# A dense layer's forward and backward pass on one core: an edge column copied on chip instead of loaded, a bias row spread by TensorE, and the orders written anew

## The chip, the core and the metric

The kernel runs on one core of a Trainium2 chip. The core has five engines with a queue each: TensorE (PE, matrix products; its weight loads are listed as PEld), VectorE (DVE), ScalarE (ACT), GpSimd (POOL) and SyncE (SP). Transfers run on 16 DMA engines and are issued from the queues of SyncE, ScalarE and GpSimd. The metric is device time in microseconds (us). Before the change three runs took 267.77, 268.63 and 269.6 us; the median is 268.63.

## The reference

x and grad_out are 2048 x 448, w1 is 448 x 1792, w2 is 1792 x 448, all in bf16. The kernel computes the layer and all its gradients:

```python
def _fwd_reference(x, w1, b1, w2, b2):
    h = jnp.einsum("bsd,df->bsf", x, w1) + b1
    h = _gelu(h)                      # tanh form
    return jnp.einsum("bsf,fd->bsd", h, w2) + b2
# reference: out, and the gradients of x, w1, b1, w2, b2 for grad_out
```

## The kernel before

The 2048 rows are cut into 4 blocks of 512, the 1792 hidden columns into 14 tiles of 128, worked on in pairs: 4 x 7 = 28 pairs, numbered p = 0 to 27. The work has two stages. The first goes through the blocks and computes the output and x's gradient; the second computes the gradients of w1 and w2 from the whole of x and grad_out. The change touches the first stage and the loads ahead of it.

No scheduler decides the order. Each engine has a written list of short names (`PE_ORDER`, `ACT_ORDER`, `DVE_ORDER`, `SP_ORDER`), and the class `Plan` turns the names into instructions in that order. Every operation names the values that it reads and writes; the waits follow from that. An engine does its list strictly in order, so an operation that waits holds up all behind it.

The names on TensorE. `W10` is ten warm-up products of constants. `h0`, `h1` are the first pair's product x w1 for the two halves of block 0. `u3.1` and `u3.2` are the two runs of the same product for pair 3, `q3.1` and `q3.2` those of grad_out w2 transposed. The last 64 of the 448 rows are folded in: a run keeps the upper and the lower 64 rows of the array busy with different halves, three slots of two products in run 1 and four in run 2. For that the first 64 numbers of each row stand a second time, in partitions 64 to 127 one column ahead of the transposed block. The transposed load fills that place with numbers of the row before; for block 0 there is none, so a small load (`+x` for x, `+g` for grad_out, function `LED`) brings the column. Run 2 of u and of q reads it. `p2.0` to `p2.3` are parts of the output of block 0 for pair 2. `o1.0.0.6.1` is a part of the output of block 1: row half 0, hidden tiles 0 to 6, run 1; `x...` is the same for x's gradient.

The names on VectorE and ScalarE. `c3A` and `c3B` move the two PSUM banks of u3 to SBUF with the bias b1, on whichever engine the list puts them. Then follow the steps of gelu and its derivative: `s` (square) and `g` (gelu) and `t` (tanh) on ScalarE, `e r y z m n` on VectorE, and `G`, which multiplies with q's result in PSUM. Since q has only one pair of banks (`qb`), the next q waits for G. `vo1.2` moves a part of the output out of PSUM and adds b2 (VectorE); `vx1.2` moves a part of x's gradient, on either engine.

The names on SyncE and ScalarE's queue for loads. `X0.0`, `X0.1`: the two halves of x's block 0, transposed; `Y0`: block 0 of grad_out; `L0` to `L3`: four column parts of w1 (256, 256, 512 and 768 columns), rows 0 to 383; `R0`, `R1`: the last 64 rows of w1; `R2`, `R3`: its first 64 rows a second time, which run 2 reads. `K0` to `K3`: parts of w2, wanted by the p parts; `J` w2 transposed, wanted by q; `I` w1 transposed, wanted by x's gradient; `b2`: the bias loaded once for each of the 128 partitions. Stores are `H`, `T` and `S`; `Nx` and `Ng` load x and grad_out for the second stage. Stores to the outputs go through three staging buffers (`stage`).

Of the kernel before, what the change touches and what calls it, by code (L numbers as in the profile page):

```python
# [88 lines left out]


PE_ORDER = """
W10 h0.0 h1.0 u1.1 u2.1 u1.2 u2.2 u3.1 p0.0 p0.1 u3.2 u4.1 p0.2 p0.3 u4.2 p1.0 p1.1 p1.2 p1.3 u5.1 p2.0 p2.1 u5.2 p2.2
p2.3 p3.0 p3.1 q0.1 p3.2 p3.3 u6.1 q0.2 u6.2 p4.0 p4.1 q1.1 p4.2 p4.3 q1.2 p5.0 p5.1 p5.2 p5.3 u7.1 q2.1 u7.2 q2.2
p6.0 p6.1 u8.1 p6.2 p6.3 u8.2 q3.1 x0.1.0.6.1 u9.1 q3.2 u9.2 x0.0.0.6.1 q4.1 u10.1 q4.2 u10.2 x0.0.0.6.2 q5.1 u11.1
q5.2 u11.2 x0.1.0.6.2 x0.0.6.10.1 u12.1 q6.1 u12.2 q6.2 x0.1.6.10.1 x0.0.6.10.2 u13.1 q7.1 u13.2 q7.2 x0.1.6.10.2
x0.0.10.14.1 q8.1 x0.1.10.14.1 u14.1 q8.2 u14.2 x0.0.10.14.2 q9.1 x0.1.10.14.2 u15.1 q9.2 u15.2 o1.0.0.6.1 q10.1 u16.1
q10.2 u16.2 o1.1.0.6.1 o1.0.0.6.2 u17.1 q11.1 u17.2 q11.2 o1.1.0.6.2 o1.0.6.10.1 o1.1.6.10.1 u18.1 q12.1 u18.2 q12.2
o1.0.6.10.2 u19.1 o1.1.6.10.2 u19.2 o1.0.10.14.1 o1.1.10.14.1 q13.1 u20.1 q13.2 u20.2 o1.0.10.14.2 o1.1.10.14.2 q14.1
x1.0.0.6.1 q14.2 x1.1.0.6.1 x1.0.0.6.2 x1.1.0.6.2 q15.1 x1.0.6.10.1 q15.2 x1.1.6.10.1 u21.1 x1.0.6.10.2 u21.2
x1.1.6.10.2 q16.1 x1.0.10.14.1 u22.1 q16.2 u22.2 x1.1.10.14.1 x1.0.10.14.2 x1.1.10.14.2 u23.1 q17.1 u23.2 q17.2  # L100
o2.0.0.6.1 o2.1.0.6.1 u24.1 q18.1 u24.2 q18.2 o2.0.0.6.2 o2.1.0.6.2 o2.0.6.10.1 o2.1.6.10.1 q19.1 u25.1 q19.2 u25.2
o2.0.6.10.2 o2.1.6.10.2 o2.0.10.14.1 o2.1.10.14.1 q20.1 o2.0.10.14.2 u26.1 q20.2 u26.2 o2.1.10.14.2 x2.0.0.6.1 q21.1
x2.1.0.6.1 q21.2 x2.0.0.6.2 u27.1 x2.1.0.6.2 u27.2 q22.1 x2.0.6.10.1 q22.2 x2.1.6.10.1 x2.0.6.10.2 x2.1.6.10.2 q23.1
x2.0.10.14.1 q23.2 x2.1.10.14.1 x2.0.10.14.2 x2.1.10.14.2 q24.1 o3.0.0.6.1 q24.2 o3.1.0.6.1 o3.0.0.6.2 o3.1.0.6.2
q25.1 o3.0.6.10.1 q25.2 o3.1.6.10.1 o3.0.6.10.2 o3.1.6.10.2 q26.1 o3.0.10.14.1 q26.2 o3.1.10.14.1 o3.0.10.14.2 q27.1
o3.1.10.14.2 q27.2 x3.0.0.6.1 x3.1.0.6.1 x3.0.0.6.2 x3.1.0.6.2 x3.0.6.10.1 x3.1.6.10.1 x3.0.6.10.2 x3.1.6.10.2
x3.0.10.14.1 x3.1.10.14.1 x3.0.10.14.2 x3.1.10.14.2
"""
ACT_ORDER = """
L0 R0 b1 table c0A0 c0A1 s0 g0 c1A t0 s1 g1 s2 g2 c4A g3 g4 t1 t2 s3 c5A g5 s4 s5 c6A g6 t3 s6 c7A t4 g7 c8A c8B g8 s7  # L110
t5 c9A c9B g9 s8 t6 c10A c10B g10 s9 t7 c11A c11B g11 s10 t8 c12A c12B g12 s11 t9 c13A c13B g13 s12 t10 c14A c14B
vx0.1 g14 s13 c15A c15B g15 t11 t12 c16A c16B g16 s14 t13 c17A s15 c17B g17 s16 t14 c18A c18B g18 s17 c19A c19B t15
g19 s18 c20A c20B g20 t16 s19 t17 s20 c21A c21B t18 g21 s21 c22A c22B vx1.0 t19 g22 vx1.3 c23A s22 c23B g23 t20 s23
c24A c24B t21 g24 s24 c25A c25B t22 g25 s25 c26A c26B t23 g26 t24 c27A s26 c27B s27 g27 t25 vx2.0 vx2.2 t26 t27 vx3.0
vx3.2
"""
DVE_ORDER = """
b1T c0B0 c0B1 e0 r0 y0 c1B z0 c2A c2B m0 c3A c3B e1 e2 r1 c4B z1 r2 y1 z2 y2 n0 c5B m1 m2 n1 n2 G0 c6B e3 r3 y3 z3 G1
m3 e4 n3 r4 y4 z4 c7B G2 m4 vo0.2 vo0.3 vo0.0 vo0.1 e5 n4 r5 y5 z5 G3 m5 e6 n5 r6 y6 z6 G4 m6 e7 n6 r7 y7 z7 G5 m7 e8
n7 r8 y8 z8 m8 G6 n8 e9 r9 y9 z9 G7 m9 e10 n9 r10 y10 z10 G8 m10 vx0.0 e11 n10 vx0.2 vx0.3 r11 G9 z11 e12 y11 r12 y12  # L120
z12 m11 G10 m12 e13 n11 r13 y13 z13 n12 m13 G11 n13 e14 r14 y14 z14 m14 n14 G12 e15 r15 y15 z15 m15 n15 G13 e16 vo1.0
vo1.1 vo1.2 vo1.3 r16 y16 z16 G14 m16 e17 n16 r17 y17 z17 m17 G15 n17 e18 r18 y18 z18 m18 n18 G16 e19 r19 y19 z19
vx1.1 vx1.2 m19 n19 G17 e20 r20 y20 z20 m20 n20 G18 e21 r21 y21 z21 m21 n21 G19 e22 r22 y22 z22 vo2.0 m22 vo2.1 G20
n22 vo2.2 vo2.3 e23 r23 y23 z23 G21 e24 m23 r24 y24 z24 n23 m24 n24 G22 e25 r25 y25 z25 m25 G23 n25 vx2.1 e26 vx2.3
r26 y26 z26 G24 m26 e27 n26 r27 y27 z27 m27 n27 G25 G26 vo3.0 vo3.1 vo3.2 vo3.3 G27 vx3.1 vx3.3
"""
# [33 lines left out]
def make_plan(tc, ctx, x, w1, b1, w2, b2, grad_out, out_0, out_1, out_2, out_3, out_4, out_5):  # L160
    nc = tc.nc
    P = 128
# [199 lines left out]
    def wake(n):  # L362
        def fn():
            for i in range(n):
                nc.tensor.matmul(bk_(0), lhsT=one[:, 0:P], rhs=one, start=True, stop=True, skip_group_check=True)
# [238 lines left out]
    for eng, order in (("ACT", ACT_ORDER), ("DVE", DVE_ORDER)):  # L604
        for t in order.split():
            k, a = t[0], t[1:]
            if k == "c":
                hf = None if a[-1] in "AB" else int(a[-1])
                a = a if hf is None else a[:-1]
                C(int(a[:-1]), "AB".index(a[-1]), eng, hf)  # L610
            elif k == "v":
                EV(a[0], *num(a[1:]), eng)
            elif k == "L":
                LW1(int(a), eng)
            elif k == "R":
                LW1R(int(a), eng)
            elif t in ("+x", "+g"):
                LED({"x": "xT", "g": "gT"}[a], 0, eng)
            elif k == "K":
                LW2(int(a), eng)  # L620
            elif t == "b1":
                dma(eng, "b1", b1n[0:NF, :], b1.rearrange("(f p) -> f p", p=P), ["b1z"], ["b1n"], 3584)
            elif t == "b1T":
                pl.op(eng, "b1T", b1_turn, ["b1n"], ["b1T"], ("tiny", 4))
            elif t == "table":
                pl.op(eng, "table", lambda: nc.scalar.activation(out=tiny[:], in_=one[:, 0:1], func=ACT.Gelu_apprx_tanh), [], ["tiny"], ("table", 1))
# [167 lines left out]
```

## Time and profile before

| | |
|---|---|
| median of three runs | 268.63 us |
| profiled execution | 269.21 us |
| its span | 267.4 us |
| mean granted TensorE clock | 0.992 |
| TensorE busy | 260.8 us (98%) |
| VectorE busy | 196.1 us (73%) |
| ScalarE busy | 128.8 us (48%) |
| chain that ended last | PE 95%, DMA 2%, SPq 2% |

The span is what the profile shows of the execution; 1.8 us of its time lie outside. The chain that ended last is followed back from the last instruction, at each step to what released it; an engine's share in it is the time in which the end of the kernel hung on that engine. A timeline row gives start, duration, engine, source line, operation, what it writes and reads, and in brackets the idle time before it with what ended it. The granted clock of TensorE is 1.00 at full speed and 0.50 at half. A line ending in "Q" (SPq, ACTq) is an engine's queue issuing a transfer.

### The profile page before, as it was taken

What the parts mean: (1) busy time and instruction counts of PE and PEld (TensorE: products, weight loads), DVE (VectorE), ACT (ScalarE), POOL (GpSimd) and SP (SyncE); (2) the same over time, 40 slices, a digit from 0 to 9 for tenths busy, and PEclk for the clock granted to TensorE, in tenths of its full rate; (3) what the DMA queues carried; (4) which work ended last, traced back from release to release, by engine and by line L of the source; (5) the groups of instructions that cost most, each with busy time, mean ns of one, the idle gap of its engine ahead of it and who ended that gap; (6) DMA issues with size and microseconds to landing.
All of it is one profiled execution on the core that took longest, in us unless ns stands there. A gap on an engine that the chain in (4) does not pass through costs nothing.

```text
span 267.4 us, 5276 instructions
## 1 busy us (share of the span) xinstructions
PE 260.8 (98%) x2156; PEld 150.5 (56%) x2156; DVE 196.1 (73%) x273; ACT 128.8 (48%) x163; POOL 15.2 (6%) x9
## 2 busy tenths in 40 slices
...
GB/s 165 281 207 200 174 162 196 91 317 241 205 289 156 237 223 162 82 192 120 78 150 146 297 140 39 247 187 107 162 174 198 192 174 170 165 214 196 69 71 34
DMA packets 121705, 46.20 MB, mean 173 GB/s; under 512 B 99054, under 2 KB 121551, under 8 KB 121680
## 3 DMA queue, kind: packets, MB, share of 16 engines
...
q0 software_dynamic: 64, 0.01, 0.0%
...
## 4 chain that ended last, share of the span: by engine, by line
PE 95%; DMA 2%; SPq 2%; issue 0%; ACT 0%
PE bank L238 47%; PE qb L238 16%; PE bank L750 12%; PE bank L696 11%; PE qb L696 5%; PE qb L750 4%; DMA w1f<-in_w_dram 2%; SPq L513 1%; SPq L501 1%; ACT w_sb L755 0%
## 5 line engine op out<-in xcount | busy, mean ns | idle before, releaser
L238 PEld LDWEIGHTS <-HG 64*128 64x128 bf16 x896 | 56.4, 94 | 31.3 <-POOLq L233 0.9
L238 PE MATMUL qb<-gT,w2Tf 64*128 64x512 bf16 x392 | 52.9, 376 | 0.0
L238 PE MATMUL bank<-xT,w1f 64*128 64x512 bf16 x364 | 50.1, 387 | 1.7 <-DMA w1f<-in_w_dram 1.7
L238 PE MATMUL bank<-w_sb,HG 64*128 64x448 bf16 x448 | 48.0, 349 | 0.0
L238 PE MATMUL bank<-w1T_sb,HG 64*128 64x448 bf16 x448 | 47.3, 349 | 0.0
L464 DVE SCALAR_TENSOR_TENSOR HG<-TR,qb 128x1024 bf16<-128x1024 bf16 x28 | 34.1, 1216 | 5.9 <-PE qb L238 5.7
L750 PEld LDWEIGHTS <-HG 128*128 128x128 bf16 x240 | 23.4, 98 | 19.2
L238 PEld LDWEIGHTS <-w1f 64*128 64x128 bf16 x378 | 22.1, 96 | 20.9 <-DMA w1f<-in_w_dram 2.5
L238 PEld LDWEIGHTS <-w2Tf 64*128 64x128 bf16 x392 | 24.2, 94 | 16.6
L449 ACT ACTIVATE TR<-TR 128x1024 bf16<-128x1024 bf16 x28 | 29.3, 1049 | 8.7 <-DVE TR L439 8.6
L696 PEld LDWEIGHTS <-gh_nat 128*128 128x128 bf16 x224 | 21.8, 98 | 20.6 <-issue 0.4
L750 PE MATMUL bank<-w2Tf,HG 128*128 128x448 bf16 (+1 forms) x176 | 32.3, 344 | 0.0
L696 PE MATMUL bank<-w1f,gh_nat 128*128 128x448 bf16 x160 | 30.8, 353 | 0.0
L719 DVE TENSOR_TENSOR w1T_sb<-w1T_sb,gh_nat 128x1792 f32<-128x1792 f32 x14 | 28.4, 2026 | 0.5
L454 DVE TENSOR_SCALAR TR<-TR 128x2048 bf16<-128x2048 bf16 x28 | 19.2, 688 | 8.2 <-ACT TR L449 8.2
L725 POOL PARTITION_ALL_REDUCE w1T_sb<-w1T_sb x1 | 10.6, 10649 | 209.5 <-DVE w1T_sb L723 209.5
L424 ACT ACTIVATE TR<-gh_nat 128x1024 bf16<-128x1024 bf16 x15 | 15.7, 1052 | 8.5 <-DVE TR L459 8.5
L406 ACT ACTIVATE ub<-bank,b1T 128x512 bf16<-128x512 f32 (+1 forms) x22 | 14.0, 673 | 11.8 <-PE bank L238 5.4
L459 DVE TENSOR_TENSOR TR<-TR 128x1024 bf16<-128x1024 bf16 x28 | 19.1, 685 | 0.3
L444 DVE TENSOR_TENSOR TR<-TR,HG 128x1024 bf16<-128x1024 bf16 x28 | 19.1, 682 | 0.0
L756 DVE CAST w_sb<-bank 128x448 bf16<-128x448 f32 x5 | 3.1, 623 | 19.9 <-PE bank L750 19.9
L701 ACT ACTIVATE TR<-bank 128x448 bf16<-128x448 f32 x10 | 5.4, 544 | 24.1 <-PE bank L696 22.0
...
## 6 DMA issues: line engine op xcount, KB each, us to landing
...
out_dram<-st SPq DMA_DIRECT2D x16, 224.0 KB, 2.4
...
out_dram<-xT SPq DMA_DIRECT2D x2, 384.0 KB, 3.0
...
w1f<-in_w_dram SPq DMA_DIRECT2D x1, 576.0 KB, 5.9
```

What stands on the lines that cost most here:

```text
L238: m = nc.tensor.matmul(bk_(b)[:, 0:n], lhsT=l, rhs=r, start=st, stop=sp, skip_group_check=True)
L406: fn = lambda: nc.scalar.activation(out=out, in_=src, func=ACT.Identity, bias=bias)
L424: pl.op("ACT", f"s{p}", lambda: nc.scalar.activation(out=TR[p % NTR][:, 1], in_=ubuf(p), func=ACT.Square, scale=sc), [("ub", p)], [v], ("a ...
L444: pl.op("DVE", f"R{p}", lambda: nc.vector.tensor_tensor(out=t[:, 1], in0=t[:, 1], in1=hblk(p), op=ALU.mult), [("r", p), ("h", p)], [val((" ...
L449: pl.op("ACT", f"t{p}", lambda: nc.scalar.activation(out=t[:, 0], in_=t[:, 0], func=ACT.Tanh), [("y", p)], [val(("t", p), ("TR0", p % NTR) ...
L454: pl.op("DVE", f"m{p}", lambda: nc.vector.tensor_scalar(out=t[:], in0=t[:], scalar1=1.0, scalar2=None, op0=ALU.subtract), [("t", p), ("r2" ...
L459: pl.op("DVE", f"n{p}", lambda: nc.vector.tensor_tensor(out=t[:, 0], in0=t[:, 0], in1=t[:, 1], op=ALU.mult), [("m0", p), ("m1", p)], [val( ...
L464: pl.op("DVE", f"G{p}", lambda: nc.vector.scalar_tensor_tensor(out=ghblk(p), in0=t[:, 0], scalar=2.0, in1=qb[:, :, :], op0=ALU.subtract, o ...
L696: nc.tensor.matmul(bk_(bk)[:, 0:D], lhsT=gh_nat[:, st // 4, ft, st % 4, :], rhs=x_nat[:, st, :], start=(st == 0), stop=(st == NS - 1))
L719: nc.vector.tensor_tensor(out=hs3, in0=a, in1=gh_nat[:, st // 4, :, st % 4, :], op=ALU.add)
L725: pl.op("POOL", "gb1", lambda: nc.gpsimd.partition_all_reduce(gb1_w, hsum, channels=P, reduce_op=bass_isa.ReduceOp.add), ["hsc"], ["gb1"], ...
L750: nc.tensor.matmul(bk_(bk)[:, 0:d1 - d0], lhsT=h_nat[ft][:, st, :], rhs=g_nat[:, st, d0:d1], start=(st == 0), stop=(st == NS - 1))
```

## The change

- `+x` and `+g` leave SyncE's list. `Dx0` and `Dg0` take their place in VectorE's list: a copy of one column of the transposed block from partitions 0 to 63 into partitions 64 to 127.
- b2 is loaded as one row of 448 numbers into the first partition of a staging buffer, from ScalarE's queue behind b1 and ahead of the table load. TensorE spreads it over 128 partitions by a product with ones (`B`, into bank 3), and VectorE copies it out of PSUM (`b2c`).
- The warm-up is nine products, then B, then one more product.
- All four lists are new. In SyncE's, L2 follows R2 directly, L3 goes behind K1, K0, R1 and R3, and Y0, J0 and X1 follow K3. In TensorE's, q0 starts after u6, the output of a block comes ahead of x's gradient of the block before, and the parts of o and x are cut in 4, 4, 3 and 3 hidden tiles instead of 6, 4 and 4. ScalarE takes nearly all first halves of u (`cA`) and all of `vx`; VectorE takes all second halves from pair 4 on (`cB`).

```diff
 PE_ORDER = """
-W10 h0.0 h1.0 u1.1 u2.1 u1.2 u2.2 u3.1 p0.0 p0.1 u3.2 u4.1 p0.2 p0.3 u4.2 p1.0 p1.1 p1.2 p1.3 u5.1 p2.0 p2.1 u5.2 p2.2
-p2.3 p3.0 p3.1 q0.1 p3.2 p3.3 u6.1 q0.2 u6.2 p4.0 p4.1 q1.1 p4.2 p4.3 q1.2 p5.0 p5.1 p5.2 p5.3 u7.1 q2.1 u7.2 q2.2
+W9 B W1 h0.0 h1.0 u1.1 u2.1 u1.2 u2.2 u3.1 p0.0 p0.1 u3.2 u4.1 p0.2 p0.3 u4.2 p1.0 p1.1 p1.2 p1.3 p2.0 u5.1 p2.1 p2.2
+u5.2 p2.3 p3.0 p3.1 p3.2 u6.1 p3.3 u6.2 q0.1 p4.0 p4.1 q0.2 p4.2 u7.1 p4.3 p5.0 u7.2 p5.1 p5.2 p5.3 u8.1 p6.0 p6.1
+u8.2 q1.1 p6.2 p6.3 q1.2 u9.1 o1.1.0.4.1 u9.2 o1.0.0.4.1 q2.1 u10.1 q2.2 u10.2 o1.0.0.4.2 q3.1 u11.1 q3.2 u11.2
...
 ACT_ORDER = """
-L0 R0 b1 table c0A0 c0A1 s0 g0 c1A t0 s1 g1 s2 g2 c4A g3 g4 t1 t2 s3 c5A g5 s4 s5 c6A g6 t3 s6 c7A t4 g7 c8A c8B g8 s7
-t5 c9A c9B g9 s8 t6 c10A c10B g10 s9 t7 c11A c11B g11 s10 t8 c12A c12B g12 s11 t9 c13A c13B g13 s12 t10 c14A c14B
+L0 R0 b1 b2 table c0A0 c0A1 s0 g0 c1A t0 s1 g1 s2 c3A g2 c4A t1 g3 s3 c5A t2 g4 s4 s5 c6A g5 g6 c7A t3 g7 s6 c8A g8
+c9A g9 t4 c10A g10 s7 t5 c11A g11 s8 c12A t6 g12 s9 c13A g13 t7 t8 c14A g14 s10 t9 c15A g15 s11 t10 c16A g16 s12 t11
...
 DVE_ORDER = """
-b1T c0B0 c0B1 e0 r0 y0 c1B z0 c2A c2B m0 c3A c3B e1 e2 r1 c4B z1 r2 y1 z2 y2 n0 c5B m1 m2 n1 n2 G0 c6B e3 r3 y3 z3 G1
-m3 e4 n3 r4 y4 z4 c7B G2 m4 vo0.2 vo0.3 vo0.0 vo0.1 e5 n4 r5 y5 z5 G3 m5 e6 n5 r6 y6 z6 G4 m6 e7 n6 r7 y7 z7 G5 m7 e8
+b1T b2c Dx0 c0B0 c0B1 e0 r0 y0 c1B c2A c2B z0 e1 c3B m0 r1 y1 c4B z1 e2 n0 m1 r2 y2 z2 c5B n1 m2 Dg0 n2 c6B G0 e3 r3
+y3 c7B z3 m3 n3 c8B vo0.2 vo0.3 vo0.0 vo0.1 G1 e4 c9B r4 y4 z4 G2 c10B m4 e5 n4 r5 y5 z5 c11B m5 G3 n5 e6 r6 y6 c12B
...
 SP_ORDER = """
-X0.0 X0.1 L1 R2 +x L2 L3 K0 K1 R3 R1 K2 J0 J1 Y0 +g K3 J2 X1 b2 I0 J3 I1 Y1 Ex Eg So0.1 So0.0 X2 H0 H1 H2 H3 H4 H5 H6
+X0.0 X0.1 L1 R2 L2 K1 K0 R1 R3 L3 K2 K3 Y0 J0 X1 J2 J1 Y1 J3 I1 I0 Ex Eg So0.1 So0.0 X2 H0 H1 H2 H3 H4 H5 H6 H7 H8 T0
...
-    def LED(tag, b, eng):
-
-        src, dst = ((x2, xT), (g2, gT))[tag == "gT"]
-        v = val((tag[0] + "e", b), (tag + "e", b % 2))
-        dma(eng, f"edge{tag}{b}", dst[b % 2][64:128, 3, EDGE - 1:EDGE], src[b * SB:b * SB + 1, 0:64].rearrange("a c -> c a"), [], [v], 128)
+    def LED(tag):
+
+        dst = {"xT": xT, "gT": gT}[tag][0]
+        v = val((tag[0] + "e", 0), (tag + "e", 0))
+        pl.op("DVE", f"edge{tag}", lambda: nc.vector.tensor_copy(out=dst[64:128, 3, EDGE - 1:EDGE], in_=dst[0:64, 0, EDGE:EDGE + 1]),
+              [(tag, 0, 0)], [v], ("tiny", 1))
...
+        elif k == "B":
+            pe("b2u", lambda: nc.tensor.matmul(bk_(3)[:, 0:D], lhsT=one[0:1, 0:P], rhs=stage[NST - 1][0:1, 0, :], start=True, stop=True,
+                                               skip_group_check=True), ["b2r"], [bank(("b2u",), 3)], ("s448", 1), (None, 0))
...
+            elif t == "b2":
+                dma(eng, "b2", stage[NST - 1][0:1, 0, :], b2.rearrange("(o d) -> o d", o=1), [], ["b2r"], D * 2)
+            elif t == "b2c":
+                pl.op(eng, "b2c", lambda: nc.vector.tensor_copy(out=b2_bc[:], in_=bk_(3)[:, 0:D]), [("b2u",)], ["b2"], ("evx", 1))
...
-        elif t == "b2":
-            dma("SP", "b2", b2_bc[:], b2.rearrange("(o d) -> o d", o=1).to_broadcast((P, D)), [], ["b2"], P * D * 2)
```

More of the change, by code (lines that the diff above doesn't have):

```diff
@@ L91 @@
 PE_ORDER = """
-W10 h0.0 h1.0 u1.1 u2.1 u1.2 u2.2 u3.1 p0.0 p0.1 u3.2 u4.1 p0.2 p0.3 u4.2 p1.0 p1.1 p1.2 p1.3 u5.1 p2.0 p2.1 u5.2 p2.2
-p2.3 p3.0 p3.1 q0.1 p3.2 p3.3 u6.1 q0.2 u6.2 p4.0 p4.1 q1.1 p4.2 p4.3 q1.2 p5.0 p5.1 p5.2 p5.3 u7.1 q2.1 u7.2 q2.2
-p6.0 p6.1 u8.1 p6.2 p6.3 u8.2 q3.1 x0.1.0.6.1 u9.1 q3.2 u9.2 x0.0.0.6.1 q4.1 u10.1 q4.2 u10.2 x0.0.0.6.2 q5.1 u11.1
-q5.2 u11.2 x0.1.0.6.2 x0.0.6.10.1 u12.1 q6.1 u12.2 q6.2 x0.1.6.10.1 x0.0.6.10.2 u13.1 q7.1 u13.2 q7.2 x0.1.6.10.2
-x0.0.10.14.1 q8.1 x0.1.10.14.1 u14.1 q8.2 u14.2 x0.0.10.14.2 q9.1 x0.1.10.14.2 u15.1 q9.2 u15.2 o1.0.0.6.1 q10.1 u16.1
@@ L97 @@
[L97 to L106, printed above, removed]
@@ L107 @@
-x3.0.10.14.1 x3.1.10.14.1 x3.0.10.14.2 x3.1.10.14.2
+W9 B W1 h0.0 h1.0 u1.1 u2.1 u1.2 u2.2 u3.1 p0.0 p0.1 u3.2 u4.1 p0.2 p0.3 u4.2 p1.0 p1.1 p1.2 p1.3 p2.0 u5.1 p2.1 p2.2
+u5.2 p2.3 p3.0 p3.1 p3.2 u6.1 p3.3 u6.2 q0.1 p4.0 p4.1 q0.2 p4.2 u7.1 p4.3 p5.0 u7.2 p5.1 p5.2 p5.3 u8.1 p6.0 p6.1
+u8.2 q1.1 p6.2 p6.3 q1.2 u9.1 o1.1.0.4.1 u9.2 o1.0.0.4.1 q2.1 u10.1 q2.2 u10.2 o1.0.0.4.2 q3.1 u11.1 q3.2 u11.2
+o1.1.0.4.2 o1.0.4.8.1 o1.1.4.8.1 u12.1 o1.0.4.8.2 u12.2 q4.1 o1.1.4.8.2 q4.2 u13.1 o1.0.8.11.1 u13.2 q5.1 o1.1.8.11.1
@@ new lines @@
+q5.2 o1.0.8.11.2 o1.1.8.11.2 o1.0.11.14.1 o1.1.11.14.1 q6.1 o1.0.11.14.2 q6.2 o1.1.11.14.2 x0.0.0.4.1 u14.1 x0.0.0.4.2
+u14.2 x0.1.0.4.1 q7.1 u15.1 q7.2 u15.2 x0.1.0.4.2 x0.0.4.8.1 q8.1 u16.1 q8.2 u16.2 x0.1.4.8.1 x0.0.4.8.2 q9.1 u17.1
+q9.2 u17.2 x0.1.4.8.2 x0.0.8.11.1 x0.1.8.11.1 x0.0.8.11.2 u18.1 x0.1.8.11.2 u18.2 q10.1 x0.0.11.14.1 q10.2 u19.1
+x0.1.11.14.1 u19.2 q11.1 x0.0.11.14.2 q11.2 u20.1 x0.1.11.14.2 u20.2 q12.1 o2.0.0.4.1 q12.2 o2.1.0.4.1 o2.0.0.4.2
+o2.1.0.4.2 o2.0.4.8.1 q13.1 o2.1.4.8.1 q13.2 o2.0.4.8.2 o2.1.4.8.2 o2.0.8.11.1 o2.1.8.11.1 q14.1 o2.0.8.11.2 q14.2
@@ new lines @@
+u21.1 o2.1.8.11.2 u21.2 q15.1 o2.0.11.14.1 q15.2 u22.1 o2.1.11.14.1 u22.2 q16.1 o2.0.11.14.2 u23.1 q16.2 u23.2
+o2.1.11.14.2 x1.0.0.4.1 u24.1 x1.0.0.4.2 u24.2 x1.1.0.4.1 q17.1 x1.1.0.4.2 q17.2 x1.0.4.8.1 x1.1.4.8.1 x1.0.4.8.2
+q18.1 x1.1.4.8.2 q18.2 x1.0.8.11.1 x1.1.8.11.1 x1.0.8.11.2 q19.1 x1.1.8.11.2 q19.2 x1.0.11.14.1 x1.1.11.14.1
+x1.0.11.14.2 u25.1 x1.1.11.14.2 u25.2 q20.1 o3.0.0.4.1 q20.2 o3.1.0.4.1 u26.1 o3.0.0.4.2 u26.2 q21.1 o3.1.0.4.2 q21.2
+o3.0.4.8.1 u27.1 o3.1.4.8.1 u27.2 q22.1 o3.0.4.8.2 q22.2 o3.1.4.8.2 o3.0.8.11.1 o3.1.8.11.1 q23.1 o3.0.8.11.2 q23.2
@@ L108 @@
+o3.1.8.11.2 o3.0.11.14.1 o3.1.11.14.1 o3.0.11.14.2 q24.1 o3.1.11.14.2 q24.2 x2.0.0.4.1 x2.1.0.4.1 x2.0.0.4.2 q25.1
+x2.1.0.4.2 q25.2 x2.0.4.8.1 x2.1.4.8.1 x2.0.4.8.2 x2.1.4.8.2 x2.0.8.11.1 x2.1.8.11.1 x2.0.8.11.2 q26.1 x2.1.8.11.2
+q26.2 x2.0.11.14.1 x2.1.11.14.1 x2.0.11.14.2 q27.1 x2.1.11.14.2 q27.2 x3.0.0.4.1 x3.1.0.4.1 x3.0.0.4.2 x3.1.0.4.2
+x3.0.4.8.1 x3.1.4.8.1 x3.0.4.8.2 x3.1.4.8.2 x3.0.8.11.1 x3.1.8.11.1 x3.0.8.11.2 x3.1.8.11.2 x3.0.11.14.1 x3.1.11.14.1
+x3.0.11.14.2 x3.1.11.14.2
 """
 ACT_ORDER = """
-L0 R0 b1 table c0A0 c0A1 s0 g0 c1A t0 s1 g1 s2 g2 c4A g3 g4 t1 t2 s3 c5A g5 s4 s5 c6A g6 t3 s6 c7A t4 g7 c8A c8B g8 s7
@@ L111 @@
-t5 c9A c9B g9 s8 t6 c10A c10B g10 s9 t7 c11A c11B g11 s10 t8 c12A c12B g12 s11 t9 c13A c13B g13 s12 t10 c14A c14B
[L112 to L115, printed above, removed]
+L0 R0 b1 b2 table c0A0 c0A1 s0 g0 c1A t0 s1 g1 s2 c3A g2 c4A t1 g3 s3 c5A t2 g4 s4 s5 c6A g5 g6 c7A t3 g7 s6 c8A g8
@@ L116 @@
+c9A g9 t4 c10A g10 s7 t5 c11A g11 s8 c12A t6 g12 s9 c13A g13 t7 t8 c14A g14 s10 t9 c15A g15 s11 t10 c16A g16 s12 t11
+c17A g17 s13 s14 c18A t12 g18 c19A g19 t13 vx0.0 vx0.1 vx0.2 c20A vx0.3 g20 s15 t14 s16 t15 s17 s18 t16 c21A g21 t17
+c22A g22 s19 t18 c23A g23 s20 t19 s21 t20 s22 c24A t21 g24 vx1.0 vx1.1 vx1.2 vx1.3 s23 c25A t22 g25 s24 c26A t23 g26
+s25 s26 c27A t24 g27 s27 t25 t26 t27 vx2.0 vx2.1 vx2.2 vx2.3 vx3.0 vx3.1 vx3.2 vx3.3
 """
 DVE_ORDER = """
-b1T c0B0 c0B1 e0 r0 y0 c1B z0 c2A c2B m0 c3A c3B e1 e2 r1 c4B z1 r2 y1 z2 y2 n0 c5B m1 m2 n1 n2 G0 c6B e3 r3 y3 z3 G1
@@ L119 @@
-m3 e4 n3 r4 y4 z4 c7B G2 m4 vo0.2 vo0.3 vo0.0 vo0.1 e5 n4 r5 y5 z5 G3 m5 e6 n5 r6 y6 z6 G4 m6 e7 n6 r7 y7 z7 G5 m7 e8
[L120 to L123, printed above, removed]
```

24 lines of the change are left out of this document (14 added, 10 removed).

## The prediction

> **What bounds the kernel now.** I read the page's first part and its chain first, then the timeline of each engine over the first 16 us, then the windows.
>
> ```profile
> PE 260.8 (98%) x2156; PEld 150.5 (56%) x2156; DVE 196.1 (73%) x273; ACT 128.8 (48%) x163; POOL 15.2 (6%) x9
> PE 95%; DMA 2%; SPq 2%; issue 0%; ACT 0%
> 5.35 4.99 DMA w1f<-in_w_dram
> 10.38 4.24 PE bank L238 x22
> ```
>
> The chain is TensorE for 95%. Its one long wait is a load that SyncE issued at 5.35 and that landed at 10.34: L2, the third column part of w1. From 10.38 to the last product nothing else stands in the chain. The windows (PE, PEld, DVE, ACT, POOL, granted clock, DMA share, GB/s) confirm it and show one more loss:
>
> ```profile
> 3.74:7.16 3.42, 2.31 (x16) 1.29 (x15) 0.86 (x5) 0.45 (x3) 0.00 (x0) 1.00 1.08 197
> 7.16:10.58 3.42, 1.74 (x14) 0.54 (x14) 1.43 (x4) 2.52 (x4) 0.00 (x0) 1.00 0.90 279
> 10.58:14.00 3.42, 3.42 (x18) 1.20 (x16) 1.49 (x3) 0.95 (x2) 0.00 (x0) 0.50 1.10 319
> 14.00:179.00 165.00, 165.00 (x1642) 101.16 (x1640) 139.37 (x226) 111.13 (x133) 0.00 (x0) 1.00 0.84 182
> 30.00:150.00 120.00, 120.00 (x1187) 72.45 (x1183) 108.10 (x176) 92.65 (x111) 0.00 (x0) 1.00 0.85 184
> ```
>
> From 14 to 179 us TensorE is busy 165.00 of 165.00 us at full clock, so no order of the same products makes that stretch shorter. Between 10.58 and 14.00 the granted clock is 0.50: 3.42 us that do 1.71 us of work. What the change can win lies ahead of 14.45, what it can lose anywhere. TensorE's own timeline of the start:
>
> ```profile
> 0.77 3.79 PE L365 MATMUL bank<-const-bfloat16-1.0 128*128 128x512 bf16 x10 [0.77 <-PEq L778]
> 5.66 1.14 PE L282 MATMUL bank<-xT,w1f 128*128 128x256 bf16 x8 [1.11 <-DMA xT<-in_x_dram]
> 6.73 1.15 PE L282 MATMUL qb<-xT,w1f 128*128 128x256 bf16 x8
> 8.71 0.82 PE L238 MATMUL bank<-xT,w1f 64*128 64x512 bf16 x6 [0.83 <-DMA w1f<-in_w_dram]
> 10.38 4.24 PE L238 MATMUL bank<-xT,w1f 64*128 64x512 bf16 x22 [0.85 <-DMA w1f<-in_w_dram]
> 14.45 0.81 PE L238 MATMUL qb<-xT,w1f 64*128 64x512 bf16 x6
> 15.10 0.92 PE L238 MATMUL bank<-w_sb,HG 64*128 64x448 bf16 x8
> ```
>
> Warm-up, wait for x, h0 and h1 (2.2 us), wait for L1, u1.1, wait for L2, then u2.1, u1.2, u2.2 at mostly half clock; u3.1 starts at 14.45. I use that start as the mark: what reaches it earlier or later moves the end by as much. At full clock six products of 512 columns take 0.65 us (14.45 to 15.10), so eight take 0.86, and u1.1, u2.1, u1.2, u2.2 together 3.02.
>
> **The change, part by part.** The queues that the edits touch (SPq, ACTq are the issue times):
>
> ```profile
> 0.73 2.69 SPq L513 DMA_TRANSPOSE xT<-in_x_dram  x2
> 3.46 1.22 SPq L501 DMA_DIRECT2D w1f<-in_w_dram  x2
> 4.73 0.58 SPq L501 DMA_DIRECT2D xT<-in_x_dram  x1
> 9.98 5.23 SPq L513 DMA_TRANSPOSE w2Tf<-in_w_dram  x2
> 15.25 2.80 SPq L513 DMA_TRANSPOSE gT<-in_grad_out_dram  x1
> 1.79 0.81 ACTq L501 DMA_DIRECT2D b1n<-in_b_dram  x1
> 2.63 1.28 ACT L626 ACT_TABLE_LOAD   x1 [2.63 <-issue]
> 6.14 0.85 DVE L598 STREAM_TRANSPOSE b1T<-b1n 32x32 bf16<-32x32 bf16 x4 [6.14 <-DMA b1n<-in_b_dram]
> 25.12 1.28 DVE L459 TENSOR_TENSOR TR<-TR 128x1024 bf16<-128x1024 bf16 x2
> ```
>
> The times from issue to landing of these loads, over the first 16 us:
>
> ```profile
> w1f<-in_w_dram SPq DMA_DIRECT2D x1, 576.0 KB, 5.9
> w_sb<-in_w_dram SPq DMA_DIRECT2D x2, 224.0 KB, 6.4
> w1f<-in_w_dram SPq DMA_DIRECT2D x1, 384.0 KB, 5.0
> w1f<-in_w_dram ACTq DMA_DIRECT2D x1, 192.0 KB, 2.8
> xT<-in_x_dram SPq DMA_DIRECT2D x1, 0.1 KB, 4.7
> xT<-in_x_dram SPq DMA_TRANSPOSE x2, 4.6
> gT<-in_grad_out_dram SPq DMA_TRANSPOSE x1, 4.9
> ```
>
> 1. *The load of 64 numbers (+x) leaves SyncE.* It held the queue from 4.73 to 5.35, so L2 is issued 0.62 earlier: 4.73 + 5.0 = 9.73. If the transfer engines are what limits it (DMA share 0.90 and 1.10 in the windows), it stays near 10.34. Range 9.73 to 10.34.
>
> 2. *b2 as one row, B in the warm-up.* ScalarE issues b2 behind b1, at about 1.79 + 0.81 = 2.6. TensorE waits for it at B, and behind B stand W1, h0 and everything else; so b2's landing is now where TensorE begins. Bounds: 2.8 as for the first load on that queue gives 5.4; b1 itself took 6.14 - 1.79 = 4.35, which gives 7.0; 5.25, as L1 took (3.46 to 8.71), gives 7.9. The second of x's two transposed loads, issued half-way between 0.73 and 3.42 at 2.1, landed after 4.6 at 6.7. I take 6.7, between its two neighbours. B (448 columns) and W1 (512) are 0.19 + 0.22 at full clock: h0 begins at 7.1, where it began at 5.66. The first two waits are lost time anyway, for L1 lands only at 8.71.
>
> 3. *The clock.* TensorE kept full clock after a stretch with 2.31 us of work and lost it after one with 1.74. Nine warm-up products end at about 4.3; with B and W1 the stretch 3.74 to 7.16 then holds some 1.0 us. I expect half clock from 7.16 to 10.58 instead of from 10.58 to 14.00. The 2.2 us of h0 and h1: 0.06 done by 7.16, 1.71 by 10.58, the last 0.43 by 11.0. Then neither L1 (8.71) nor L2 (at most 10.34) is waited for: u3.1 at 11.0 + 3.02 = 14.0. Against 14.45: **0.4 us won**.
>
> The windows are as long as the Trainium skill says in "TensorE: Matmul & The Clock Gate", section "What's actually happening" (about 3.4 us, free-running; 3.42 here). But it gives half clock after an idle window, and the stretch before the loss held 1.74 us of products: there the trace disagrees. By that rule no half clock would follow 7.16; this is rival 1.
>
> 4. *Loads in a new order.* L3 goes behind K1, K0, R1 and R3: five places of 0.62 behind 4.73, issued at 7.8, landed at 13.7 (5.9) to 14.2 (6.4). u4.1 wants it after u3.1, two output parts (0.76) and u3.2: 14.0 + 0.65 + 0.76 + 0.86 = 16.3, or 14.6 if the clock stays up. Hidden by 2 us, or by 0.4. K0 (6.0 + 6.4 = 12.4) is wanted at 14.7. Cost nothing; without that cover TensorE waits for L3, and u4.1 is late by the difference.
>
> 5. *VectorE's copies.* b2's copy out of PSUM (about 0.62, as the other 448-column passes below) and x's column (64 numbers, under 0.2) run between 6.9 and 7.8, where VectorE waits for h0. u1.2 wants the column at 12.3. g's copy stands in VectorE's queue ahead of n2 (the second of the two products at 25.12) and waits for the first block of g. That load moves up to SyncE's place 13, which began at 9.98: landed by 14.9, or by 20.2 if only as late as before (15.25 + 4.9). Hidden by at least 4 us; were it later, everything on VectorE would stand behind it. The table load slips by 0.6 to 4.5, unneeded before 9. The old 112 KB load of b2 was waited for by nobody.
>
> 6. *Evictions.* By form, with count, busy us and mean ns:
>
> ```profile
> L406 ACT ACTIVATE gh_nat<-bank,b1T 128x512 bf16<-128x512 f32 x24 | 15.4, 677 | 2.5 <-PE bank L238 2.5
> L406 ACT ACTIVATE ub<-bank,b1T 128x512 bf16<-128x512 f32 x21 | 13.5, 682 | 8.8 <-PE bank L238 5.4 <-DVE TR L439 3.4
> L408 DVE TENSOR_SCALAR gh_nat<-bank,b1T 128x512 bf16<-128x512 f32 x4 | 3.0, 744 | 0.0
> L486 ACT ACTIVATE st<-bank 128x448 bf16<-128x448 f32 x7 | 3.8, 543 | 21.9 <-PE bank L238 21.9
> L488 DVE TENSOR_SCALAR st<-bank 128x448 bf16<-128x448 f32 x9 | 5.4, 618 | 8.5 <-PE bank L238 8.4
> L454 DVE TENSOR_SCALAR TR<-TR 128x2048 bf16<-128x2048 bf16 x28 | 19.2, 688 | 8.2 <-ACT TR L449 8.2
> 14.72 1.40 DVE L408 TENSOR_SCALAR ub<-bank,b1T 128x512 bf16<-128x512 f32 x2
> ```
>
> ScalarE did 45 full evictions of u, VectorE 9; by the new lists it is 26 and 28, and all 16 of x's gradient go to ScalarE (VectorE had 9). VectorE: 19 x 0.70 (two in a row took 1.40) - 9 x 0.62 = +7.7 us; ScalarE: -19 x 0.68 + 9 x 0.54 = -8 us. Between 30 and 150 us VectorE gets 18 of the new evictions (c8B to c25B) and loses 5 old ones (three of vx0, two of vx1): 108.1 + 12.6 - 3.1 = 117.6 of 120 us. It still fits under TensorE, so I take 0; but only 2.4 us are left (rival 3). The cuts of the output units (4, 4, 3, 3 for 6, 4, 4) change no column count.
>
> **Sum.** The profiled execution took 269.21 (span 267.4): 269.21 - 0.4 = 268.8. It stands 0.58 above the median of the three runs, 268.63, whose spread (267.77 to 269.6) is as wide as one half-clock window costs; from the median it would be 268.2. I take the middle, **268.5**, as the likeliest, its own range 267.7 to 269.3. Within 1% (2.7 us) is about what a measurement of this kernel can tell from no change.
>
> **Rivals.**
> *1. The clock stays up.* h0 from 7.1 to 9.3, u1.1 to 9.95, u2.1 at 9.95 or with L2 at 10.34, u3.1 at 12.3 to 12.7: 1.8 to 2.1 us won, 267.1 to 267.4, from the median lower: 267.0. For it: how the window falls may differ per run, as the spread hints. Against: only 1.0 us of work in the stretch before.
> *2. b2 is late; TensorE gains nothing.* Landed at 7.9, B and W1 at half clock end at 8.7, h0 and h1 at 11.8, u3.1 at 14.9: 0.4 lost, 269.0 to 269.6, say 269.3. For it: L1's 5.25. Against: b2 is issued 0.8 before L1, on another queue.
> *3. VectorE becomes the bound: slower.* The tanh waits (8.2 us in the L454 row) stay, and 117.6 + 8.2 = 125.8 us must fit in 120: 5.8 lost, 274.3. It decides from the point where VectorE's waits between 30 and 150 pass 2.4 us, first seen as TensorE waiting for G (qb) or for the second half of an eviction. Against: ScalarE has 8 us less there, so tanh comes sooner.
> *4. Faster by over 1%.* b2 at 5.4 and L1 and L2 each about 1 us sooner: h0 and h1 done at 8.0, u3.1 at 11.0, 3.4 won, 265.8. Nothing in the rows makes L1 earlier.
>
> **How the numbers follow.** Forecast 0.52; rival 1 0.20, rival 2 0.15, rival 3 0.10, rival 4 0.03. The first three cases lie within 1%, less 0.02 of rival 1 whose median could fall lower and 0.01 of rival 2 with L3 late as well: faster 0.05, same 0.84, slower 0.11. The range, 266.8 to 270.2, holds the forecast and rivals 1 and 2; it ends 0.2 below the one and 0.6 above the other's upper value, for the bounds of L2 and L3 (0.6 and 0.5 us apart). Rivals 3 and 4 are left out.
>
> **What would show it.** Right: B near 6.7 after an idle of over 2 us; one half-clock window that begins near 7 and ends near 10.6; no wait of TensorE for w1f; u3.1 near 14.0; TensorE busy without a gap from there to 179; VectorE near 98% between 30 and 150. Wrong: B after 7.5 (step 2); full clock throughout (step 3); a wait for w1f at u4.1 (step 4); VectorE waiting for gT near 25 (step 5); TensorE waiting for VectorE in the long stretch (step 6).

## The result, and the profile after

The changed kernel takes 270.88 us (median; seven runs, 269.75 to 271.69), the kernel before in the same comparison 267.81. The ratio is 1.0101, with the interval [1.007, 1.0131]: slower by 1%. Ratios and their intervals compare means over all executions, here and below; the times beside them are medians. The prediction, 268.5 with a range of 266.8 to 270.2, missed it.

The profiled execution took 271.01 with a span of 269.2. The page's first part and its chain:

```profile
PE 262.0 (97%) x2157; PEld 161.5 (60%) x2157; DVE 202.6 (75%) x286; ACT 121.3 (45%) x153; POOL 15.2 (6%) x9
PE 91%; DVE 3%; ACT 2%; DMA 1%; ACTq 1%; issue 0%
```

The chain went through TensorE for 95%; now 5% of it, some 15 us, lie on VectorE and ScalarE. In order of time (shown in part) they lie between 10.85 and 26.34, behind b2's load, B, h0 and h1:

```profile
2.63 3.74 DMA st<-in_b_dram
7.49 1.82 PE bank L285 x8
...
11.88 1.07 ACT TR L427
...
18.39 0.58 ACT gh_nat L409
...
19.00 0.75 DVE gh_nat L411
...
26.34 2.07 PE bank L241 x18
```

The windows show that nothing is lost in the long stretch:

```profile
7.16:10.58 3.42, 3.42 (x18) 1.77 (x18) 1.19 (x3) 0.47 (x1) 0.00 (x0) 1.00 0.92 281
30.00:150.00 120.00, 120.00 (x1186) 79.55 (x1182) 116.50 (x190) 82.81 (x97) 0.00 (x0) 1.00 0.78 173
```

From 30 to 150 TensorE is busy 120.00 of 120.00 us, as before. TensorE's timeline of the start (shown in part) has the loss:

```profile
0.77 4.00 PE L368 MATMUL bank<-const-bfloat16-1.0 128*128 128x512 bf16 x9 [0.77 <-PEq L786]
6.42 0.53 PE L589 MATMUL bank<-st,const-bfloat16-1.0 1*128 1x448 bf16 x1 [1.65 <-DMA st<-in_b_dram]
7.28 2.03 PE L285 MATMUL bank<-xT,w1f 128*128 128x256 bf16 x8
9.24 1.47 PE L285 MATMUL qb<-xT,w1f 128*128 128x256 bf16 x7
...
13.47 1.01 PE L241 MATMUL qb<-xT,w1f 64*128 64x512 bf16 x6
14.12 1.59 PE L241 MATMUL bank<-w_sb,HG 64*128 64x448 bf16 x8
15.38 1.19 PE L241 MATMUL qb<-xT,w1f 64*128 64x512 bf16 x8
16.49 0.82 PE L241 MATMUL bank<-xT,w1f 64*128 64x512 bf16 x6
...
18.75 2.07 PE L241 MATMUL bank<-w_sb,HG 64*128 64x448 bf16 x20
22.00 0.82 PE L241 MATMUL bank<-xT,w1f 64*128 64x512 bf16 x6 [1.17 <-DVE gh_nat L411]
...
24.26 1.69 PE L241 MATMUL bank<-w_sb,HG 64*128 64x448 bf16 x16
26.34 0.82 PE L241 MATMUL bank<-xT,w1f 64*128 64x512 bf16 x6 [0.38 <-DVE gh_nat L411]
```

u3.1 starts at 13.47, 0.98 us earlier than before. Then four stretches between starts take longer than their products need at full clock (448 columns 0.189 us for a pair, 512 columns 0.216): 14.12 to 15.38 takes 1.26 for 0.76; 15.38 to 16.49 takes 1.11 for 0.86; 18.75 to 22.00 takes 3.25 for 1.89; 24.26 to 26.34 takes 2.08 for 1.51. Together 2.7 us are lost, 1.7 net; the last product ends at 266.1 instead of 264.4. Only 1.6 of the 2.7 show as idle time. The rest hides in the long durations of the rows at 14.12 and 15.38, and at the end of the rows at 18.75 and 24.26, since the profile models where a product ends.

ScalarE's and VectorE's timelines of this kernel say who was late:

```profile
10.85 0.47 ACT L409 ACTIVATE ub<-qb,b1T 128x256 bf16<-128x256 f32 x1 [1.25 <-PE qb L285]
11.36 0.48 DVE L411 TENSOR_SCALAR ub<-qb,b1T 128x256 bf16<-128x256 f32 x1 [1.53 <-ACT ub L409]
11.88 1.06 ACT L427 ACTIVATE TR<-ub 128x1024 bf16<-128x1024 bf16 x1 [0.55 <-DVE ub L411]
12.97 0.43 DVE L432 TENSOR_SCALAR TR<-TR 128x1024 bf16<-128x1024 bf16 x1 [1.12 <-ACT TR L427]
14.38 2.06 DVE L411 TENSOR_SCALAR ub<-bank,b1T 128x512 bf16<-128x512 f32 x3
17.35 1.04 ACT L427 ACTIVATE TR<-ub 128x1024 bf16<-128x1024 bf16 x1
18.29 0.67 ACT L409 ACTIVATE gh_nat<-qb,b1T 128x512 bf16<-128x512 f32 x1
19.00 0.75 DVE L411 TENSOR_SCALAR gh_nat<-qb,b1T 128x512 bf16<-128x512 f32 x1 [1.62 <-ACT gh_nat L409]
21.20 0.74 DVE L411 TENSOR_SCALAR gh_nat<-bank,b1T 128x512 bf16<-128x512 f32 x1
```

The rows of the kernel before that answer to them:

```profile
7.92 0.48 DVE L408 TENSOR_SCALAR ub<-qb,b1T 128x256 bf16<-128x256 f32 x1 [0.33 <-PE qb L282]
8.44 0.47 ACT L406 ACTIVATE ub<-qb,b1T 128x256 bf16<-128x256 f32 x1 [0.87 <-DVE ub L408]
8.95 1.06 ACT L424 ACTIVATE TR<-ub 128x1024 bf16<-128x1024 bf16 x1
16.93 1.41 DVE L408 TENSOR_SCALAR gh_nat<-qb,b1T 128x512 bf16<-128x512 f32 x2 [0.21 <-PE qb L238]
19.19 0.69 ACT L406 ACTIVATE gh_nat<-bank,b1T 128x512 bf16<-128x512 f32 x1 [0.35 <-PE bank L238]
19.26 0.74 DVE L408 TENSOR_SCALAR gh_nat<-bank,b1T 128x512 bf16<-128x512 f32 x1
```

Two things differ. The first square (s0), with which ScalarE's work begins, starts at 11.88 instead of 8.95, because h1 ended near 10.8 instead of 7.9; from there to 19 ScalarE has no gap. VectorE is late with it: its first step of gelu waits for s0 until 12.97, and behind it stand c1B, c2A and c2B (14.38 to 16.44). The second output part needs a bank that c1B empties, and u4.1 the two of c2A and c2B: it starts at 16.49, where it would have started near 15.7 without a wait.

And c3B on VectorE (19.00) waited 1.62 us for c3A on ScalarE (18.29), which stands behind s2 (17.35). Before, both were on VectorE (16.93). The wait for ScalarE is written into the program as a semaphore: c3A and c3B read the two banks of one PSUM tile, `qb`. c4A and c4B read two tiles, and in the rows of before they run side by side on two engines (19.19 and 19.26). c0A1 and c0B1 read `qb`, and they run one after the other (7.92 and 8.44). That the shared tile is what orders them is read from these pairs. Behind c3B on VectorE stood m0, r1, y1 and c4B (21.20), and for c4B TensorE waited at 22.00.

So there are two theories. **A**: c3A on ScalarE holds c3B. **B**: TensorE stands idle until b2 is there, h0 and h1 run at half clock (2.03 us for eight products, 1.14 before), and the gelu chain (the steps `s`, `e` and so on behind each pair) starts 2.9 us late. The rival **C** is the prediction's third: VectorE, with 97% between 30 and 150, is the bound.

### The profile page after: what moved, and what is told of

Read it like the earlier page. It is cut to its first block, busy times and chain, and to the rows that moved or that the text cites. A ratio compares the mean times of both kernels' runs of the same rounds, so it can differ in the third digit from the quotient of the medians.

```text
span 269.2 us, 5316 instructions
## 1 busy us (share of the span) xinstructions
PE 262.0 (97%) x2157; PEld 161.5 (60%) x2157; DVE 202.6 (75%) x286; ACT 121.3 (45%) x153; POOL 15.2 (6%) x9
## 3 DMA queue, kind: packets, MB, share of 16 engines
HBM read 7.16 MB, written 14.27 MB: 80 GB/s over the span
## 4 chain that ended last, share of the span: by engine, by line
PE 91%; DVE 3%; ACT 2%; DMA 1%; ACTq 1%; issue 0%
PE bank L241 42%; PE qb L241 16%; PE bank L758 12%; PE bank L704 11%; PE qb L704 4%; PE qb L758 4%; DMA st<-in_b_dram 1%; ACT TR L427 1%; DVE gh_nat L411 1%; PE bank L285 1%; DVE TR L442 1%; ACTq L505 1%; PE qb L285 1%; DVE TR L457 0%; DVE TR L447 0%; DVE TR L437 0%
## 5 line engine op out<-in xcount | busy, mean ns | idle before, releaser
L241 PEld LDWEIGHTS <-HG 64*128 64x128 bf16 x896 | 62.1, 94 | 26.9 <-POOLq L236 0.8
L241 PE MATMUL qb<-gT,w2Tf 64*128 64x512 bf16 x392 | 53.7, 376 | 0.0
L241 PE MATMUL bank<-w_sb,HG 64*128 64x448 bf16 x448 | 51.6, 349 | 0.1
L241 PE MATMUL bank<-xT,w1f 64*128 64x512 bf16 x364 | 49.1, 376 | 1.6 <-DVE gh_nat L411 1.6
L241 PE MATMUL bank<-w1T_sb,HG 64*128 64x448 bf16 x448 | 48.2, 349 | 0.0
L241 PEld LDWEIGHTS <-w2Tf 64*128 64x128 bf16 x392 | 27.0, 94 | 13.4
L241 PEld LDWEIGHTS <-w1f 64*128 64x128 bf16 x378 | 24.2, 94 | 16.9 <-issue 2.5
L427 ACT ACTIVATE TR<-gh_nat 128x1024 bf16<-128x1024 bf16 x15 | 15.8, 1055 | 10.8 <-DVE TR L462 10.6
L427 ACT ACTIVATE TR<-ub 128x1024 bf16<-128x1024 bf16 x13 | 13.7, 1055 | 10.5 <-DVE TR L462 9.9
L742 DVE TENSOR_TENSOR ub<-ub,w2Tf 128x448 f32<-128x448 f32 x14 | 16.4, 1172 | 0.5
```

What stands on the lines that cost most here:

```text
L241: m = nc.tensor.matmul(bk_(b)[:, 0:n], lhsT=l, rhs=r, start=st, stop=sp, skip_group_check=True)
L427: pl.op("ACT", f"s{p}", lambda: nc.scalar.activation(out=TR[p % NTR][:, 1], in_=ubuf(p), func=ACT.Square, scale=sc), [("ub", p)], [v], ("a ...
L742: nc.vector.tensor_tensor(out=gsum, in0=gsum, in1=g_nat[:, st, :], op=ALU.add)
```

## Experiments

### One eviction moved back

An eviction is a move out of PSUM, such as c3A.

```diff
 ACT_ORDER of the changed kernel
-... s1 g1 s2 c3A g2 c4A ...
+... s1 g1 s2 g2 c4A ...
 DVE_ORDER
-... z0 e1 c3B m0 ...
+... z0 e1 c3A c3B m0 ...
```

> The changed kernel (270.88) with one eviction moved back: c3A on VectorE ahead of c3B, as before the change. Theory A (shared bank pair): c3A on ScalarE and c3B on VectorE read the two banks of qb and are put in order, so VectorE stood 1.62 us behind a busy ScalarE; with both on VectorE that wait is gone, u5.1 starts about 1.2 us sooner, 269.6 us. Theory B (late start of the gelu chain, since h0 and h1 wait for b2 and then run at half clock): nothing of that is touched, 270.9 +- 0.3. Theory C (VectorE is the bound from 30 to 150 us): one more eviction there, 270.9 to 271.3.

269.27 us (ten runs, 267.93 to 270.19); ratio to before 1.004, [1.0011, 1.0069]. TensorE's timeline has u5.1 0.3 us behind the output parts, and one wait of 0.38 is left:

```profile
18.30 2.07 PE L241 MATMUL bank<-w_sb,HG 64*128 64x448 bf16 x20
20.49 0.82 PE L241 MATMUL bank<-xT,w1f 64*128 64x512 bf16 x6
24.83 0.82 PE L241 MATMUL bank<-xT,w1f 64*128 64x512 bf16 x6 [0.38 <-DVE gh_nat L411]
```

Theory A holds. The medians differ by 1.6 us, while the ten runs lie 2.3 us apart; in the two traces u5.1 comes 8.53 us after u3.1 with c3A on ScalarE (13.47 to 22.00) and 7.38 with it on VectorE (13.11 to 20.49), 1.15 less. C said no gain, and there was one. The eviction moved lies at 17 us, though, ahead of the stretch from 30 to 150; what speaks against C there is TensorE's 120.00 of 120.00 us above.

### More warm-up ahead of B

```diff
-W9 B W1 h0.0 h1.0 ...
+W14 B W1 h0.0 h1.0 ...
```

> The changed kernel with 14 warm-up products ahead of B instead of 9: TensorE stays busy from 0.8 to about 6.6, until b2 is there. Theory B, half-clock part: the clock is full by 7.2, eight products of h0 take about 1.1 us instead of 2.0, the gelu chain starts about 1.7 us sooner, 269.2 us. Theory A alone: VectorE still waits for c3A behind s2; 270.4 to 270.9. Theory C: 270.9.

269.55 us (ten runs, 269.29 to 269.79); ratio to before 1.0059, [1.0038, 1.008], 1.3 us less than the changed kernel. TensorE's and VectorE's rows:

```profile
0.77 5.74 PE L368 MATMUL bank<-const-bfloat16-1.0 128*128 128x512 bf16 x14 [0.77 <-PEq L786]
6.96 1.14 PE L285 MATMUL bank<-xT,w1f 128*128 128x256 bf16 x8
...
17.36 0.75 DVE L411 TENSOR_SCALAR gh_nat<-qb,b1T 128x512 bf16<-128x512 f32 x1 [1.62 <-ACT gh_nat L409]
```

h0 takes 1.14 us instead of 2.03, at nearly the same start (6.96, 7.28). The wait for c3A stays at 1.62. So the half clock, not the wait for b2 itself, is what theory B is about.

### b2 loaded as before

```diff
-W9 B W1 h0.0 ...            (PE)    -L0 R0 b1 b2 table (ACT)   -b1T b2c Dx0 (DVE)   -Y0 J0 X1 J2    (SP)
+W10 h0.0 ...                        +L0 R0 b1 table            +b1T Dx0             +Y0 J0 X1 b2 J2
```

> The changed kernel with the b2 part undone: b2 loaded on 128 partitions from SyncE behind X1, ten warm-up products in a row, no B and no b2c. Theory B: h0 starts when x has landed (5.7), h1 ends near 8 to 9 and the gelu chain starts 2 to 3 us sooner; the wait for c3A stays: 268.8 to 269.2 us. Theory A alone: 270.4 to 270.9. Theory C: 270.9.

269.29 us (ten runs, 268.89 to 270.97); ratio to before 1.0044, [1.0015, 1.0074], 1.6 us less than the changed kernel, a little above what B expected. It starts h0 at 5.37, and yet u2.1 starts at 10.46, as with the fill (10.41): nothing is won by not waiting for b2. TensorE stands idle there for 1.08 us ahead of u1.1, for w1, and 0.71 ahead of u2.1, which the profile puts down to VectorE; in the next run the two waits are 0.65 and 0.82, both for w1.

### Both edits

This is the changed kernel with the first and the third edit.

> Both of the last edits: c3A on VectorE and b2 as before. Theories A and B together: both waits are gone, 267.4 to 268.0 us, as before the change or 0.3 us under it. Either one alone leaves about 269. Theory C: 269.5 or more, since VectorE has the same load between 30 and 150 us.

268.19 us (ten runs, 267.9 to 269.8); ratio to before 1.0004, [0.9975, 1.0033]. TensorE's rows have the waits for w1, and u5.1 (19.24) without a wait:

```profile
8.79 0.82 PE L241 MATMUL bank<-xT,w1f 64*128 64x512 bf16 x6 [0.65 <-DMA w1f<-in_w_dram]
10.43 2.55 PE L241 MATMUL bank<-xT,w1f 64*128 64x512 bf16 x22 [0.82 <-DMA w1f<-in_w_dram]
...
19.24 0.81 PE L241 MATMUL bank<-xT,w1f 64*128 64x512 bf16 x6
```

Over all executions the two edits undo the loss: each alone takes away 1.6 us, both 2.7. They may not undo all of it. The executions fall in two groups, and 7 of these ten lie at 267.9 to 268.42 (median 268.01), where 17 of the 31 of before lie at 267.31 to 268.05 (median 267.59). Between these, 0.4 us are left, and their cause is open. Theory C's 269.5 or more did not come, though VectorE has the evictions of the new lists between 30 and 150 us.

With c3A moved back and the 14 warm-up products, b2 staying a row:

> The changed kernel with c3A on VectorE and with 14 warm-up products ahead of B; b2 stays one row spread by TensorE. If the two causes add (-1.6 for c3A, -1.3 for the fill): 268.0 us, as before the change. If B's wait for b2 itself costs beyond the half clock: 268.8 or more.

268.35 us (eleven runs, 268.03 to 268.71); ratio 1.0012, [0.9991, 1.0032]. Against the faster group of before beside it (22 of 33, median 267.77), 0.6 us are left, where 0.4 were left with b2 loaded as before. So the b2 row itself costs at most some 0.2 us once TensorE has products to do until shortly before it lands, and none of the eleven is near 269.4.

### The parts alone, on the lists of before

c3A put on ScalarE behind s2, nothing else:

> The kernel before (267.97) with nothing changed but c3A, which goes to ScalarE behind s2. Theory A: VectorE stands behind it for 0.8 to 1.5 us near 17 us; u5.1 had 0.5 us to spare, so 0.4 to 1.0 us are lost: 268.4 to 269.0. If the shared bank pair only hurts where h0 and h1 were late: 267.9 to 268.1.

268.88 us against 267.93; ratio 1.0041, [1.0012, 1.0069]. VectorE's and TensorE's rows:

```profile
17.43 0.75 DVE L408 TENSOR_SCALAR gh_nat<-qb,b1T 128x512 bf16<-128x512 f32 x1 [1.77 <-ACT gh_nat L406]
...
19.90 0.82 PE L238 MATMUL bank<-xT,w1f 64*128 64x512 bf16 x6 [0.66 <-DVE gh_nat L408]
```

The wait of 1.77 is a little longer than expected, and the loss is what was expected. The same wait appears in a kernel that has nothing else of the change.

The b2 part alone (row behind b1, W9 B W1, b2c):

> The kernel before with only the b2 part of the change: b2 as a row behind b1, W9 B W1, b2c on VectorE; no other list changed. Theory B: h0 begins near 6.9 and at half clock, the gelu chain begins 2 to 3 us later; as between the runs with and without it on the new lists (269.27 and 268.19), 1.1 us lost: 269.1 us. If the old lists have slack for it: 268.0.

269.32 us (eleven runs, 267.66 to 269.81) against 267.93; ratio 1.0031, [1.0007, 1.0055]. The means lie closer than the medians, since a third of the executions of before are themselves near 269.4. The old lists have no slack for it either. That h0 would run at half clock did not come in the profiled execution (268.48): h0 took 1.14 us there, and the half clock began at 7.96, under h1.

The column copies alone, with +x and +g gone:

> The kernel before with only the column copies: +x and +g gone, Dx0 and Dg0 on VectorE. Upper bound of the prediction's step 1: L2 lands 0.6 us sooner, 267.4 us. Transfer engines as the limit (L2 landed at 10.4 in the other runs although it was issued at 4.7): 267.8 to 268.1 us.

268.18 us against 267.93; ratio 1.0021, [0.9994, 1.0048]: no change that can be told. In its trace the 384 KB of L2 took 5.8 us to land, and u2.1 started at 10.61.

### Can the start be made shorter?

Four more products of constants between h1 and u1.1 of the kernel before:

```diff
-W10 h0.0 h1.0 u1.1 ...
+W10 h0.0 h1.0 W4 u1.1 ...
```

> The kernel before with four more products of constants between h1 and u1.1, where TensorE waits 0.8 us for L1. Theory B, half-clock part: executions of the kernel before fall in two groups, near 267.7 and near 269.4, because the stretch with both waits for w1 sometimes costs the clock; filled, that stretch keeps it and all executions lie near 267.6, the median 0.3 us lower than before. If the clock is not decided by how busy TensorE was: two groups as before, and up to 0.1 us later.

267.78 us; ratio 0.9984, [0.9966, 1.0001]. All twelve executions lie between 266.89 and 267.91. Of the 23 of the kernel before beside them, 16 lie between 267.45 and 268.11 and 7 between 269.27 and 269.57. The upper group is gone; the median is 0.1 lower, not 0.3, and the interval just reaches 1.

```profile
7.75 1.05 PE L365 MATMUL bank<-const-bfloat16-1.0 128*128 128x512 bf16 x4
9.06 0.82 PE L238 MATMUL bank<-xT,w1f 64*128 64x512 bf16 x6 [0.27 <-DMA w1f<-in_w_dram]
10.59 2.55 PE L238 MATMUL bank<-xT,w1f 64*128 64x512 bf16 x22 [0.70 <-DMA w1f<-in_w_dram]
```

The 22 products from u2.1 take 2.55 us, where the profile of before had 4.24.

The fillers, the column copies and L2 issued ahead of R2:

> The same fillers, and the column copies of the change on the lists of before, and L2 issued ahead of R2. L2's 384 KB then stand ahead of R2's 128 KB (0.4 us at the rate of the transfer engines) and 0.6 us of issue time is gone: u2.1 starts 0.4 to 1.0 us sooner than at 10.4, 266.7 to 267.3 us, under both kernels. If L2 is held by something else: 267.6, as with the fillers alone.

267.82 us; ratio 0.9984, [0.9965, 1.0004]. All twelve executions lie between 267.15 and 268.22, without an upper group again. L2 was no earlier, against the expectation: issued near 4.1, it took 6.8 us to landing, and u2.1 started at 10.95. The transfers pause in the meantime. The window from 6 to 7 us (the last two columns are DMA share and GB/s) for the kernel before, the changed one, and this one:

```profile
6.00:7.00 1.00, 1.00 (x10) 0.54 (x8) 0.81 (x4) 0.00 (x0) 0.00 (x0) 1.00 0.83 104
```
```profile
6.00:7.00 1.00, 0.58 (x2) 0.13 (x2) 0.75 (x4) 0.00 (x0) 0.00 (x0) 1.00 0.56 68
```
```profile
6.00:7.00 1.00, 0.85 (x7) 0.38 (x5) 0.81 (x5) 0.00 (x0) 0.00 (x0) 1.00 0.13 9
```

All twelve profiled runs have this pause: 9 to 104 GB/s from 6 to 7 us, and 269 to 373 from 8 to 9. Why is open.

## Why the prediction was wrong

**Step 6, the evictions, failed: the missing term.** It counted the moved evictions as load (VectorE 117.6 of 120 us; measured 116.50, TensorE without a gap) and took 0. It did not ask what an eviction that changes its engine waits for. c3A and c3B read one tile, so on two engines they run one after the other, and the later one takes its engine's whole list with it. The term that was put at nothing measured 1.1 to 1.6 us on the changed lists and 1.0 on the old ones. The sign stood in the rows of before: the other pair that reads qb, c0A1 and c0B1, was already in order on two engines, ScalarE waiting 0.87 us for VectorE.

**Step 3, the clock, was right on where TensorE would be and wrong on the end.** h0 and h1 ran at half clock and u3.1 came at 13.47 (said 14.0). In the profiled execution the clock was not lost at 7.16, though; it had not come yet: nine warm-up products took 4.00 us, 0.43 apart to the last, where the last three of ten were fast before, and B took 0.53 us (0.34 in the run with c3A moved back, whose h0 then slowed down as forecast). The products of h1 are 0.21 us apart up to 10.1, where the first of h0 in the run with c3A moved back are 0.11 apart. The forecast of half clock under h0 and h1 came true, then, by another way in this execution. But the mark was badly chosen. "What reaches u3.1 earlier moves the end by as much" holds only if nothing else follows from h0 and h1, and ScalarE's chain does. Before, the half clock lay under u2.1, u1.2 and most of u2.2, after the chain had started; now it lies ahead of it. A step that moves a loss earlier must be followed on every engine behind it. Undoing it gave 0.9 to 1.6 us, where the prediction had 0.4 won.

**The sum's base failed as well.** The profiled execution of before, 269.21, belonged to the upper of the two groups, the one with a half-clock window that costs 1.7. I took the middle between it and a median of three; over all runs the median is 267.8 to 268.0. In the later comparisons 55 of 87 executions of before have a granted clock of 0.998 to 1.000, the other 32, near 269.4, one of 0.992 to 0.994. So most executions of before show no half clock, and the step that weighed one half-clock window against another had nothing to win there. This error hid part of the miss: from 267.8 the same sum would have given 267.4. The spread of the three runs hinted at it. The sum also takes 1% for about what a measurement can tell from no change; the interval of the result, 1.007 to 1.0131, tells less than that.

**Step 1**: L2 was issued 0.6 sooner and landed no sooner, the pessimistic bound. The reason given for that bound, busy transfer engines, is not shown: their share in the changed kernel was 0.56 from 6 to 7 us. **Step 2** was right: b2 landed at 6.4 (said 6.7). **Step 4** was right: no wait for L3. **Step 5** was right on the cost: b2c took 0.62 at 7.09 and the column copy 0.15 at 7.75; g's first block landed 10.1 us after its issue at 10.33, at 20.4, just behind the later bound (20.2), and its copy ran at 27.5 without waiting for it.

**Rivals.** Rival 3 named the right side and the right sign (TensorE waiting for the second half of an eviction) with the wrong mechanism, and for a later stretch. Rival 2 did not come: b2 was there at 6.4. Rivals 1 and 4 did not come either; the fill brought rival 1's clock, and even then, with c3A moved back as well, only the level of before. The rule of the Trainium skill ("TensorE: Matmul & The Clock Gate", section "What's actually happening") is half clock after an idle window of about 3.4 us. By it the kernel before would have kept the clock, since its longest wait behind the warm-up is 1.11 us; the trace disagrees, and the fillers, which end its upper group by filling 0.8 us, say that a window need not be wholly idle.
